# An attention part whose TensorE work stands in one fixed pattern per chunk

## The chip, the cores and the metric

The kernel runs on one core of a Trainium2 chip. The metric is device time in microseconds (us), the median of several runs; lower is better. PE is TensorE, DVE VectorE, ACT ScalarE, POOL GpSimd, SP SyncE, which issues nearly all DMAs.

## The reference

Attention over 4 batches, 8 heads, 768 positions and head dimension 64, and a feed-forward layer behind it. A query sees the 96 positions up to its own and the first 8 (the numbers come as inputs), with a penalty by distance whose slope depends on the head:

```
scores = q k^T / 8 - slope[h] * dist        (dist = 96 for a global key that is not local)
scores = where(is_global | is_local, scores, -1e9)
a = exp(scores - max); a = a / (sum(a) + 1e-9)
x = a v                                      (4*768 tokens x 512)
h = x w_in                                   (512 x 2048)
out = (gelu(h)) w_out                        (2048 x 512)
```

The weights come as float64 and are turned into pairs of 32-bit numbers on the chip.

## The kernel before

The program has two parts. The first does the attention, the weights' conversion, and the feed-forward layer for 2 of the 8 slices of 256 hidden units; the second does the other 6 slices with a seven-product scheme (lines 553 and 611). The change is in the first.

The attention goes in 12 chunks of 256 queries, three per batch; the first of a batch is narrow (its first 128 queries see one block of keys), the others wide. A chunk has four pairs of heads. Each step is an entry of a list with a letter, and this is the way of a pair p of chunk c, with its heads h:

- `l` loads q, k and v (tile `nat`); `S` (PE, line 226) makes the scores of both heads. Its matmuls contract over 64 rows of the array, one head on each half. It takes two PSUM banks, one per head.
- `R` (DVE, line 243) adds the penalty and takes the row extreme (`nmax`), out of PSUM into `pn`; `E` (ACT, line 256) is the exponential with its sums; `U` (DVE, lines 262 and 264) is the inverse of the sums (`ninv`); `N` multiplies by it, on DVE, POOL (line 274) or ACT (line 272).
- `T` (PE, line 283) turns the head's blocks with a matmul against the identity, "flips" below; `C` copies the turned blocks out of PSUM (`pt`), on ACT or DVE.
- `A` (PE, line 304) multiplies with v, each head in 64 columns of the array. Two pairs share one bank. `X` and `Y` split the result into a high and a low part (`xh`, `xl`).
- `m` (PE, line 438; line 450 in chunk 0) is the first feed-forward product, 12 matmuls an entry and four entries a chunk; it writes an `h` bank per slice. `G` is the GELU on ACT, `K` its low part on DVE. `n` (PE, line 474) is the second product, 6 matmuls an entry and four a chunk, into two `o` banks; `O` copies those out.
- Beside this run the weights' steps `w`, `D`, `F`, `j`, `J`, `H`, `L`, `Q`, `h`, `o`, `B` (load, low bits, shift, join, round, high and low parts, sums, store), on ACT, DVE, POOL and SP.

The trace shows each matmul of `S` and of `A` as two records, so a pair's scores are 8 records and its V products 16 (12 in a narrow chunk).

What sets the order: `schedule()` plans all entries at build time, with a duration for each engine written in the list. It always places the entry that can start first; on PE, entries that are ready within `SLACK` of each other go by a key (`KEYS`, by chunk and pair), on the other engines by due times with small shifts (`NUDGE`, `BIAS`). There are 8 PSUM banks, shared by the classes `ks` (scores), `kt` (flips), `ka` (V products), `kh` and `ko`; `CAP` says how many a class may hold, `KEEP` how many the planner leaves free for each of the others. The result is one order for all instructions, in which each engine's instructions are then written; on the chip, an engine that waits holds up all that is behind it. In the second part the keys of PE's entries are `strict`: they go in just that order.

Of the kernel before, what the change touches and what calls it, by code (L numbers as in the profile page):

```python
# [26 lines left out]
NST = 8  # L27
# [37 lines left out]
def slope(h):  # L65
# [10 lines left out]
BIAS = {("POOL", "N"): -0.649, ("POOL", "J"): -0.767, ("POOL", "L"): -0.258, ("POOL", "Q"): -0.723, ("POOL", "o"): 0.987, ("POOL", "D"): 0.298,  # L76
        ("ACT", "C"): -0.32, ("ACT", "X"): -0.532, ("ACT", "D"): -0.292, ("ACT", "H"): -0.564, ("ACT", "O"): 0.599, ("ACT", "N"): -0.47}
BIAS_FRONT = {("POOL", "N"): -0.845, ("POOL", "J"): -0.4, ("POOL", "L"): -0.546, ("POOL", "Q"): -0.235, ("POOL", "o"): -0.065, ("POOL", "D"): -0.221,
              ("ACT", "C"): -0.331, ("ACT", "X"): -1.028, ("ACT", "D"): -1.155, ("ACT", "H"): -0.348, ("ACT", "O"): -0.845, ("ACT", "N"): -0.4}
# [9 lines left out]
NUDGE = {("E", 1): -4.66, ("U", 1): 0.08, ("N", 2): -0.21, ("C", 0): 1.4, ("C", 2): -9.57, ("X", 2): 0.57,  # L89
         ("X", 3): -3.65, ("Y", 2): -3.14, ("K", 0): -1.28, ("K", 3): 2.23, ("H", 0): 2.88, ("L", 0): 1.38,  # L90
         ("D", 1): 1.2}
DEC = {(s, i): 57.774 + 7.137 * (4 * (s - NA) + i) for s in range(NA, NST) for i in range(4)}
EARLY_KEYS = {("A", 1): -0.91, ("m", 2): -0.43}
KEYS = {
    "S": lambda g: g + -1.051 + EARLY_KEYS.get(("S", g // 4), 0.0),
    "T": lambda g: g + 0.62 + EARLY_KEYS.get(("T", g // 4), 0.0),
    "A": lambda g: g + 2.296 + EARLY_KEYS.get(("A", g // 4), 0.0),
    "m": lambda c, s: 4 * c + 5.994 + 0.626 * s + EARLY_KEYS.get(("m", c), 0.0),
    "n": lambda c, s: 4 * c + 8.948 + 0.4 * s + EARLY_KEYS.get(("n", c), 0.0),
}  # L100
# [12 lines left out]
class Fast:  # L113
# [559 lines left out]
    def first_part(self):  # L673
# [2 lines left out]
            op(("P", h), [("DVE", .37), ("POOL", .54)], lambda e, h=h: self.penalties(e, h), [("lim",)], port=True)  # L676
        op(("lim",), ("DVE", 1.6), lambda e: self.reach_of_limits(), [("l", 0, 0)], free=[("nat", (0, 0))], port=True)
        lag = KEYS
        for c in range(NCH):
            f = c % CPB == 0  # L680
            for p in range(NP):
                g = 4 * c + p
                y = [("Y", c, p // 2)] if c >= 2 else [("Y", c, p)]
                op(("l", c, p), ("SP", ISSUE), lambda e, c=c, p=p: self.load(c, p), alloc=[("nat", (c, p))],
                   kb=(384, 640)[not f])
                op(("S", c, p), ("PE", (1.06, .86)[f]), lambda e, c=c, p=p: self.scores(c, p), [("l", c, p)],
                   alloc=[("k", ("s", c, 2 * p)), ("k", ("s", c, 2 * p + 1))], key=lag["S"](g))
                for h in (2 * p, 2 * p + 1):
                    op(("R", c, h), ("DVE", (.7, .56)[f]), lambda e, c=c, h=h: self.reduce(c, h), [("S", c, p), ("P", h)],
                       alloc=[("pn", (c, h))], free=[("k", ("s", c, h))])  # L690
                    op(("E", c, h), ("ACT", (.986, .88)[f]), lambda e, c=c, h=h: self.exps(c, h), [("R", c, h)])
                if p % UNITE == UNITE - 1:
                    q = p - UNITE + 1
                    op(("U", c, p // UNITE), ("DVE", .29), lambda e, c=c, q=q: self.inverse(c, q),
                       [("E", c, h) for h in range(2 * q, 2 * p + 2)])
                for h in (2 * p, 2 * p + 1):
                    op(("N", c, h), [("DVE", (.53, .47)[f]), ("POOL", (1.0, .85)[f]), ("ACT", (.8, .71)[f])],
                       lambda e, c=c, h=h: self.scale(e, c, h), [("U", c, p // UNITE)], port=True)
                    op(("T", c, h), ("PE", (.4, .29)[f]), lambda e, c=c, h=h: self.flip(c, h), [("N", c, h)],
                       alloc=[("k", ("t", c, h))], free=[("pn", (c, h))], key=lag["T"](g) + .001 * (h % 2))  # L700
# [3 lines left out]
                op(("A", c, p), ("PE", (1.02, .77)[f]), lambda e, c=c, p=p: self.av_pair(c, p),  # L704
                   [("C", c, 2 * p), ("C", c, 2 * p + 1), ("l", c, p), self.at("A", c, p - 1)],
                   alloc=([("k", ("a", c, p // 2))] if p % 2 == 0 else []) + ([("x", c)] if p == 0 else []),
                   free=[("pt", (c, 2 * p)), ("pt", (c, 2 * p + 1)), ("nat", (c, p))], key=lag["A"](g))
# [54 lines left out]
        for c in range(NCH):  # L762
            for s in range(NA):
# [6 lines left out]
                           free=[("x", c)], key=lag["m"](c, s) + (.01 * p if s else .6 * (p - 3)))  # L770
                    continue
                for f in range(2):
                    op(("m", c, s, f), ("PE", 1.5), lambda e, c=c, s=s, f=f: self.m1(c, s, f),
                       ys + [("L", s, 0), ("L", s, 1), self.at("m", c, s, 0)] , alloc=[("k", ("h", c, s))] if f == 0 else [],
                       free=[("x", c)], key=lag["m"](c, s) + .01 * f)
            for batch in BATCH(c):
                op(("G",) + batch[0], ("ACT", 1.02 * len(batch)), lambda e, batch=batch: self.gelu(batch),
                   [("m",) + b + (3 if c < SPLIT else 1,) for b in batch], alloc=[("g", b) for b in batch])
# [1 line left out]
                    op(("K",) + b, ("DVE", .6), lambda e, b=b: self.gelu_low(*b), [("G",) + batch[0]], free=[("k", ("h",) + b)])  # L780
            for s in range(NA):
                for k in range(2):
                    op(("n", c, s, k), ("PE", 1.4), lambda e, c=c, s=s, k=k: self.m2(c, s, k),
                       [("K", c, s), ("L", s, 2), ("L", s, 3), ("H", s, 3), self.at("n", c, s - 1, k)],
                       alloc=[("k", ("o", c, k))] if s == 0 else [], free=[("g", (c, s))], key=lag["n"](c, s) + .01 * k)
# [210 lines left out]
    def schedule(self):  # L996
# [95 lines left out]
                make_ready(i)  # L1092
        self.start, self.on = [None] * n, [None] * n
        port = pipe = 0.0
        self.uses_port = uses_port = lambda o, e: e == "POOL" or e == "DVE" and o.port
        while len(done) < n:
            best = None
            for e in engines:
                found, low = [], None
                k = 0  # L1100
                for i in ready[e]:
# [16 lines left out]
                    if low is None or t < low:  # L1118
                        low = t
                    found.append((t, i))  # L1120
# [311 lines left out]
```

## Time and profile before

| | us |
|---|---|
| median of 3 runs (669.45 to 670.78) | 669.74 |
| the profiled execution | 670.06 |
| its span, first to last instruction | 668.30 |
| PE busy in the span | 647.85 |
| first product of the second part starts at | 288.85 |

The span is what the trace covers; the profiled execution's time has another 1.8 us around it. The starts of PE's instructions are measured, their ends modelled: a row's busy time can reach past the next row's start.

### The profile page before, as it was taken

How to read it: one execution, taken by the hardware profiler on the slowest of the kernel's cores; microseconds unless marked ns; L12 is line 12 of the kernel's file. 1: busy time of each engine (PE TensorE's matmuls, PEld its weight loads, DVE VectorE, ACT ScalarE, POOL GpSimd, SP SyncE). 2: the span in 40 equal slices, each digit the busy share in tenths (PEclk: the TensorE clock that was granted, in tenths of full speed). 3: DMA queues.
4: the chain of work that ended last, by engine and by line, in shares of the span. 5: the costliest groups of instructions: out<-in, count | busy, mean ns of one | idle time of the engine just before them, and what ended most of it. 6: DMA issues, size and time to landing. Idle time of an engine off the chain costs nothing. (4 is left out here: it accounts for less than half of the span.)

```text
span 668.3 us, 14910 instructions
## 1 busy us (share of the span) xinstructions
PE 647.9 (97%) x5356; PEld 593.7 (89%) x5356; DVE 544.7 (82%) x1562; ACT 443.5 (66%) x1146; POOL 178.1 (27%) x216
## 2 busy tenths in 40 slices
PE   8999999999999999999999999999999999999994
PEld 6778878777887887899999999999999999999994
DVE  8998799999899977366588879778977987897784
ACT  6999999899999988445554465456445545644450
POOL 5667776765786553200000000000000000000002
PEclk9999999999999999999999999999999999999998
DMA  8876798689898869969997879688888979787302
GB/s 317 286 234 198 284 380 301 246 305 366 304 367 310 306 257 402 375 236 351 416 405 265 290 276 389 216 310 310 314 303 290 344 251 334 266 283 248 115 1 69
DMA packets 48753, 192.44 MB, mean 288 GB/s; under 512 B 5408, under 2 KB 5920, under 8 KB 41760
## 3 DMA queue, kind: packets, MB, share of 16 engines
q1 hardware_dynamic: 48384, 191.16, 78.0%
q8 instruction: 44, 0.72, 0.4%
q14 instruction: 37, 0.30, 0.1%
q10 hardware_dynamic: 288, 0.26, 0.1%
HBM read 150.50 MB, written 40.89 MB: 286 GB/s over the span
## 5 line engine op out<-in xcount | busy, mean ns | idle before, releaser
L611 PE MATMUL k<-w,go 128*128 128x256 f32 x1512 | 193.9, 282 | 1.7 <-DVE vw L620 0.8
L611 PEld LDWEIGHTS k<-w,go 128*128 128x128 f32 x1512 | 185.1, 189 | 3.0 <-PE k L553 1.6
L553 PE MATMUL k<-xch,w1a 128*128 128x256 f32 x576 | 110.4, 284 | 0.5 <-DVE hc L563 0.5
L620 POOL TENSOR_TENSOR part<-part,r 128x256 f32<-128x256 f32 x1 | 0.7, 740 | 372.3 <-DVE r L620 372.3
L256 ACT ACTIVATE pn<-pn,nmax 128x256 f32<-128x256 f32 (+1 forms) x192 | 91.8, 480 | 7.0 <-DVE nmax L243 6.7
L553 PEld LDWEIGHTS k<-xch,w1a 128*128 128x128 f32 x576 | 92.5, 191 | 1.0 <-DVE hc L563 0.7
L553 PE MATMUL k<-xch,w1b 128*128 128x256 f32 x432 | 91.4, 282 | 0.5 <-ACT hc L559 0.5
L559 ACT COPY hc<-k 128x256 f32<-128x256 f32 x108 | 39.8, 369 | 68.0 <-PE k L553 67.6
L553 PE MATMUL k<-xcl,w1a 128*128 128x256 f32 x288 | 81.4, 283 | 0.0
L563 DVE TENSOR_TENSOR hc<-hc,k 128x256 f32<-128x256 f32 x108 | 45.0, 417 | 36.1 <-ACT hc L559 26.3
L595 ACT CAST go<-gb 128x384 fp32r<-128x384 f32 x72 | 36.9, 513 | 55.6 <-PE k L611 55.3
L553 PEld LDWEIGHTS k<-xch,w1b 128*128 128x128 f32 x432 | 73.1, 191 | 0.7 <-ACT hc L559 0.7
L243 DVE CUSTOM_DVE_ANT_0 pn<-k,pens 128x256 f32<-128x256 f32 (+1 forms) x192 | 65.7, 395 | 7.5 <-PE k L226 6.6
L571 ACT ACTIVATE gb<-hc 128x256 f32<-128x256 f32 x108 | 45.2, 419 | 40.0 <-DVE hc L563 39.0
L553 PE MATMUL k<-xcl,w1b 128*128 128x256 f32 x216 | 60.9, 282 | 0.0
L272 ACT ACTIVATE pn<-pn,ninv 128x256 f32<-128x256 f32 (+1 forms) x118 | 50.0, 484 | 10.8 <-DVE ninv L264 10.5
L194 DVE TENSOR_TENSOR go<-gb,go 128x384 fp32r<-128x384 f32 x72 | 40.0, 555 | 19.7 <-ACT go L595 19.3
L283 PE MATMUL k<-ident,pn 128*128 128x128 f32 x352 | 51.5, 279 | 4.3 <-DVE pt L191 1.6
L553 PEld LDWEIGHTS k<-xcl,w1a 128*128 128x128 f32 x288 | 55.1, 191 | 0.0
L354 POOL TENSOR_TENSOR wa<-wa,ws 128x512 int32<-128x512 int32 x32 | 44.2, 1383 | 35.9 <-DVE wa L349 15.4
L226 PE MATMUL k<-nat 64*128 64x256 f32 (+1 forms) x384 | 50.8, 384 | 2.8 <-ACT pt L191 0.8
L438 PE MATMUL k<-xh,winh 128*128 128x256 f32 x176 | 52.3, 297 | 0.8 <-DVE xl L194 0.8
(122 smaller groups left out, 1464.1 us busy)
## 6 DMA issues: line engine op xcount, KB each, us to landing
w1a<-w1d SPq DMA_DIRECT2D x36, 1024.0 KB, 7.4
w1b<-w1d SPq DMA_DIRECT2D x36, 768.0 KB, 5.1
nat<-qkv SPq DMA_DIRECT2D x32, 640.0 KB, 5.9
ws<-w SPq DMA_DIRECT2D x32, 512.0 KB, 5.4
c<-w SPq DMA_DIRECT2D x64, 256.0 KB, 5.3
w1d<-wst SPq DMA_DIRECT2D x6, 1792.0 KB, 6.7
w2d<-wst SPq DMA_DIRECT2D x6, 1792.0 KB, 6.5
nat<-qkv SPq DMA_DIRECT2D x16, 386.0 KB, 4.6
```

What stands on the lines that cost most here:

```text
L194: self.eng(e).tensor_tensor(out=out, in0=in_, in1=hi.bitcast(F32), op=ALU.subtract)
L226: self.nc.tensor.matmul(sp[hh][:, j, :w], lhsT=qq[hr, j * P:(j + 1) * P], rhs=kt[hr, 0 if first else j, :w], start=True, stop=True)
L243: self.nc.vector.tensor_tensor_reduce(out=nn[:, j, :w], in0=sp[:, j, :w], in1=pen, scale=-0.125, scalar=3e38, op0=ALU.add, op1=ALU.min, ac ...
L256: self.nc.scalar.activation(out=nn[:, j, :w], in_=nn[:, j, :w], func=AF.Exp, bias=self.nmax[:, k, i:i + 1], scale=-1.0, accum_out=self.nsu ...
L272: self.nc.scalar.activation(out=nn[:, j, :w], in_=nn[:, j, :w], func=AF.Copy, scale=by)
L283: self.nc.tensor.transpose(tp[:, i, :], nn[:, j, a * P:(a + 1) * P], self.ident)
L354: self.eng(e).tensor_tensor(out=a, in0=a, in1=self.t["ws", (s, i)][:, :, 0], op=ALU.add)
L438: nc.tensor.matmul(hp[:, f, :], lhsT=w[:, d, f * P:(f + 1) * P], rhs=x[:, d, :], start=n == 0, stop=n == 3 * NP - 1)
L553: self.nc.tensor.matmul(out, lhsT=w[:, i, d * P:(d + 1) * P], rhs=y[:, d, :], start=bool(new) and n == 0, stop=n == 5, skip_group_check=no ...
L563: self.nc.vector.tensor_tensor(out=x, in0=x, in1=self.t["k", (bank, u)], op=ALU.add)
L571: self.nc.scalar.activation(out=out, in_=src, func=AF.Gelu)
L611: self.nc.tensor.matmul(out[k], lhsT=o[:, i, a], rhs=w[:, b, j], start=s == 0 and n == 0 and k in (1, 4, 5, 6), stop=s == NB - 1 and n == ...
```

## The change

It does four things to the planner and none to the matmuls. `turn(x, y)` gives a time that PE loses between an entry of kind x and one of kind y; the planner adds it to an entry's earliest start on PE, and the durations of S, T, A, m and n in the list become smaller. `SEATS` gives each S, T, A, m and n a place in a chunk's period of 4, and in the keys from 10.086 to 44.882 (`STEADY`) these entries are strict. `KEEP` becomes zero throughout and scores may hold four banks. The tables of shifts have new numbers (only some are shown).

```diff
-CAP = {"ks": 2, "kt": 3, "ka": 2, "kh": 2, "ko": 2, "kb": 4}
-KEEP = {"ks": 1, "kt": 1, "ka": 1, "kh": 1, "ko": 3}
+CAP = {"ks": 4, "kt": 3, "ka": 2, "kh": 2, "ko": 2, "kb": 4}
+KEEP = {"ks": 0, "kt": 0, "ka": 0, "kh": 0, "ko": 0}
...
-FRONT = 26.926
-SPLIT, CHECK, UNITE, RING = 1, 8, 1, 3
+FRONT = 8.503
+SPLIT, CHECK, UNITE, RING, GREED = 1, 8, 1, 3, 0.0
+STEADY = (10.086, 44.882)
+SEATS = {"S": [-2.0, -1.84, 0.0, 0.16],
+         "T": [0.4, 0.48, 0.56, 0.64, 1.85, 2.56, 2.64, 2.93],
+         "A": [1.6, 1.76, 3.6, 3.76],
+         "m": [4.45, 4.53, 4.61, 4.69],
+         "n": [7.2, 7.28, 7.44, 8.44]}
...
-DEC = {(s, i): 57.774 + 7.137 * (4 * (s - NA) + i) for s in range(NA, NST) for i in range(4)}
+DEC = {(s, i): 57.774 + 6.435 * (4 * (s - NA) + i) for s in range(NA, NST) for i in range(4)}
...
+def turn(x, y):
+    if x == y:
+        return .08 if x == "T" else 0.0
+    if x == "T":
+        return {"S": .175, "A": .175, "m": .07, "n": .11}.get(y, .08)
+    if x in ("S", "A"):
+        return {"S": .2, "A": .1}[x] + {"T": .055, "m": .09, "n": .125}.get(y, 0.0)
+    if x in ("m", "n"):
+        return {"S": .09, "A": .09}.get(y, 0.0)
+    return 0.0
...
+        def seat(kind, c, k, free):
+            at = 4 * c + SEATS[kind][k]
+            return dict(key=at, strict=True) if STEADY[0] <= at < STEADY[1] else dict(key=free)
+
...
-                op(("S", c, p), ("PE", (1.06, .86)[f]), lambda e, c=c, p=p: self.scores(c, p), [("l", c, p)],
-                   alloc=[("k", ("s", c, 2 * p)), ("k", ("s", c, 2 * p + 1))], key=lag["S"](g))
+                op(("S", c, p), ("PE", (.86, .66)[f]), lambda e, c=c, p=p: self.scores(c, p), [("l", c, p)],
+                   alloc=[("k", ("s", c, 2 * p)), ("k", ("s", c, 2 * p + 1))], **seat("S", c, p, lag["S"](g)))
...
-                op(("A", c, p), ("PE", (1.02, .77)[f]), lambda e, c=c, p=p: self.av_pair(c, p),
+                op(("A", c, p), ("PE", (.92, .71)[f]), lambda e, c=c, p=p: self.av_pair(c, p),
...
+                    if e == "PE":
+                        base = max(base, free[e] + turn(turned, o.name[0]))
...
+                    late = GREED * turn(turned, o.name[0]) if e == "PE" else 0.0
...
+            if e == "PE":
+                turned = o.name[0]
```

With these numbers the order of PE changes throughout the first part. In a seated chunk it is now: two pairs of S, three flips, three n, two pairs of A, two pairs of S, a flip, the last n, then m and a flip in turn (m, T, m, T, m, T, m), two pairs of A, a flip. Before, the chunks differ from each other. The first place is PE at the second V products of a chunk, with `k` the PSUM banks, `nat` the loaded pair, `pn` the scaled exponentials and `pt` their turned copies. Before, where chunk 3 ends and chunk 4's scores stand:

```order
L304 MATMUL k_1371<-pt_1379,nat_1035 64x128
...
L304 MATMUL k_1371<-pt_1396,nat_1035 64x128
L226 MATMUL k_1429<-nat_1314 128x256
L226 MATMUL k_1430<-nat_1314 128x256
L226 MATMUL k_1429<-nat_1314 128x256
L226 MATMUL k_1430<-nat_1314 128x256
L283 MATMUL k_1442<-ident,pn_1343 128x128 x4
L474 MATMUL k_1383<-wouth_644,gh_1_1306 128x512
```

One pair of A, one pair of S, a flip, and an entry of n. Now, at the like place (the lines are 20 or so further down in the changed file: 246 is S, 303 T, 324 A, 494 n):

```order
L324 MATMUL k_1422<-pt_1340,nat_989 64x128
...
L324 MATMUL k_1422<-pt_1411,nat_998 64x128
L246 MATMUL k_1449<-nat_1322 128x256
L246 MATMUL k_1450<-nat_1322 128x256
L246 MATMUL k_1449<-nat_1322 128x256
L246 MATMUL k_1450<-nat_1322 128x256
L246 MATMUL k_1460<-nat_1324 128x256
L246 MATMUL k_1461<-nat_1324 128x256
L246 MATMUL k_1460<-nat_1324 128x256
L246 MATMUL k_1461<-nat_1324 128x256
L303 MATMUL k_1471<-ident,pn_1349 128x128 x4
L494 MATMUL k_1388<-wouth_594,gh_1_1309 128x512
```

Two pairs of A (`nat_989` and `nat_998`) and two pairs of S stand together, and four banks of scores are open at once. The second place is PE at a block of scores near entries of n. Before, a pair of chunk 4 stands behind an entry of n, ahead of flips and m:

```order
L474 MATMUL k_1402<-wouth_644,gh_1_1306 128x512
L226 MATMUL k_1491<-nat_1351 128x256
L226 MATMUL k_1492<-nat_1351 128x256
L226 MATMUL k_1491<-nat_1351 128x256
L226 MATMUL k_1492<-nat_1351 128x256
L283 MATMUL k_1503<-ident,pn_1398 128x128 x4
L283 MATMUL k_1513<-ident,pn_1413 128x128 x4
L438 MATMUL k_1521<-xh_1292,winh_463 128x256
```

Now, at the first two pairs of chunk 5, the block has two pairs again, with flips on both sides and three entries of n in a run behind them:

```order
L303 MATMUL k_1644<-ident,pn_1487 128x128 x4
L246 MATMUL k_1650<-nat_1444 128x256
L246 MATMUL k_1651<-nat_1444 128x256
...
L246 MATMUL k_1661<-nat_1455 128x256
L246 MATMUL k_1662<-nat_1455 128x256
L303 MATMUL k_1675<-ident,pn_1494 128x128 x4
L303 MATMUL k_1681<-ident,pn_1517 128x128 x4
L303 MATMUL k_1689<-ident,pn_1549 128x128 x4
L494 MATMUL k_1697<-wouth_468,gh_0_1619 128x512
```

What moved: S and A pairs of a chunk have come together in twos, and the flips between m and m are one at a time. From the first product of the second part on, PE's rows are the same in both.

## Rows read from the trace of the kernel before

**Rows 1.** Busy time by stretch: from:to, length, each engine (records), clock, DMA share, GB/s.
```profile
0.00:62.50 62.50, 57.94 (x487) 46.59 (x489) 56.28 (x206) 54.84 (x155) 40.46 (x60) 1.00 0.75 256
62.50:253.90 191.40, 186.73 (x1548) 151.89 (x1548) 173.98 (x506) 179.42 (x488) 125.18 (x140) 1.00 0.84 313
253.90:288.80 34.90, 34.80 (x282) 29.92 (x277) 20.94 (x58) 22.33 (x59) 8.88 (x12) 1.00 0.97 371
288.80:668.30 379.50, 368.39 (x3051) 365.27 (x3050) 293.48 (x796) 186.87 (x446) 3.56 (x5) 0.99 0.75 273
sum 668.30, PE 647.85 PEld 593.67 DVE 544.68 ACT 443.47 POOL 178.08; mean PE 161.96 PEld 148.42 DVE 136.17 ACT 110.87 POOL 44.52
```

**Rows 2.** Timeline of PE: start, busy us, line, output and inputs, array, shape, records.
```profile
4.70 1.58 PE L226 MATMUL k<-nat 64*128 64x128 f32 x16
6.99 0.93 PE L226 MATMUL k<-nat 64*128 64x128 f32 x8 [0.71 <-DMA nat<-qkv]
...
101.45 0.36 PE L438 MATMUL k<-xh,winh 128*128 128x256 f32 x1
...
102.97 0.60 PE L283 MATMUL k<-ident,pn 128*128 128x128 f32 x4
103.32 0.36 PE L438 MATMUL k<-xh,winh 128*128 128x256 f32 x1
...
104.93 1.14 PE L226 MATMUL k<-nat 64*128 64x256 f32 x8
106.00 1.09 PE L304 MATMUL k<-pt,nat 128*64 128x128 f32 x16
107.02 1.09 PE L283 MATMUL k<-ident,pn 128*128 128x128 f32 x8
108.04 1.14 PE L226 MATMUL k<-nat 64*128 64x256 f32 x8
...
110.13 0.50 PE L474 MATMUL k<-wouth,gh 128*128 128x512 f32 x1
...
110.93 0.40 PE L474 MATMUL k<-wouth,gh 128*128 128x512 f32 x1
...
182.87 1.97 PE L304 MATMUL k<-pt,nat 128*64 128x128 f32 x32
...
283.10 0.28 PE L438 MATMUL k<-xh,winh 128*128 128x256 f32 x1
...
288.85 0.28 PE L553 MATMUL k<-xch,w1a 128*128 128x256 f32 x1
```

**Rows 3.** Groups by line and shape, 62.5 to 253.9: busy us, mean ns, idle before.
```profile
L272 ACT ACTIVATE pn<-pn,ninv 128x256 f32<-128x256 f32 x75 | 33.7, 499 | 5.0 <-DVE ninv L264 4.9
L339 ACT ACTIVATE ws<-ws 128x512 int32<-128x512 uint32 x17 | 11.2, 672 | 0.0
L191 ACT COPY pt<-k 128x512 f32<-128x512 f32 x15 | 8.3, 578 | 1.1 <-PE k L283 1.1
L243 DVE CUSTOM_DVE_ANT_0 pn<-k,pens 128x256 f32<-128x256 f32 x106 | 39.8, 416 | 4.7 <-PE k L226 4.2 <-ACT pn L256 0.3 <-PE k L283 0.2
L191 DVE COPY pt<-k 128x512 f32<-128x512 f32 x27 | 18.0, 682 | 2.8 <-PE k L283 2.8
L400 DVE TENSOR_TENSOR wst<-wa,wst 128x512 fp32r<-128x512 f32 x7 | 7.0, 999 | 0.0
L274 POOL TENSOR_SCALAR pn<-pn,ninv 128x256 f32<-128x256 f32 x29 | 14.8, 521 | 16.3 <-DVE ninv L264 8.4 <-ACT pn L256 5.6 <-PE k L226 2.0
```

**Rows 4.** Busy time by stretch, two chunks, columns as in rows 1.
```profile
136.10:160.30 24.20, 21.77 (x185) 17.48 (x185) 23.16 (x69) 21.91 (x64) 13.05 (x14) 1.00 0.89 340
183.60:207.70 24.10, 24.10 (x218) 20.07 (x216) 23.38 (x67) 23.83 (x64) 16.59 (x18) 1.00 0.88 340
```

**Rows 5.** Waits of ACT, 62.5 to 253.9: us in total, times, longest.
```profile
ACT pn L272 <- DVE ninv L264: 8.5, 10, 1.8
```

**Rows 6.** Waits of PE, 136.1 to 160.3.
```profile
PE k L283 <- DVE pt L191: 1.4, 2, 0.9
```

More of the change, by code (lines that the diff above doesn't have):

```diff
@@ L72 @@
          "hc1": 2, "hc6": 2, "hc5": 2, "gb0": 5, "gb1": 7, "gx": 2}
-CAP = {"ks": 2, "kt": 3, "ka": 2, "kh": 2, "ko": 2, "kb": 4}
-KEEP = {"ks": 1, "kt": 1, "ka": 1, "kh": 1, "ko": 3}
+CAP = {"ks": 4, "kt": 3, "ka": 2, "kh": 2, "ko": 2, "kb": 4}
+KEEP = {"ks": 0, "kt": 0, "ka": 0, "kh": 0, "ko": 0}
 SOON, SLACK, WINDOW, LAT, LAT0, IDLE = 0.0, 0.1, 12, 0.255, .05, 19.761
[L76 to L79, printed above, removed]
-FRONT = 26.926
-SPLIT, CHECK, UNITE, RING = 1, 8, 1, 3
+BIAS = {("POOL", "N"): -1.029, ("POOL", "J"): -0.767, ("POOL", "L"): 0.15, ("POOL", "Q"): -0.723, ("POOL", "o"): 0.987, ("POOL", "D"): 0.852,
+        ("ACT", "C"): -0.32, ("ACT", "X"): -0.657, ("ACT", "D"): -0.292, ("ACT", "H"): -0.564, ("ACT", "O"): 0.279, ("ACT", "N"): -0.527}
+BIAS_FRONT = {("POOL", "N"): -0.807, ("POOL", "J"): -0.4, ("POOL", "L"): -0.546, ("POOL", "Q"): -0.235, ("POOL", "o"): -0.065, ("POOL", "D"): -0.221,
+              ("ACT", "C"): -0.331, ("ACT", "X"): -1.028, ("ACT", "D"): -1.155, ("ACT", "H"): -0.479, ("ACT", "O"): -0.845, ("ACT", "N"): -0.256}
+FRONT = 8.503
[6 more added lines that the diff above has]
+         "n": [7.2, 7.28, 7.44, 8.44]}
 W2_AFTER = {(3, 1): ("p", 1, 1), (4, 0): ("p", 1, 4), (4, 1): ("p", 2, 4), (5, 0): ("p", 3, 4), (5, 1): ("p", 4, 4)}
@@ L88 @@
 FREE = (3.4, 2.5, 3.0, 2.0, .8)
-NUDGE = {("E", 1): -4.66, ("U", 1): 0.08, ("N", 2): -0.21, ("C", 0): 1.4, ("C", 2): -9.57, ("X", 2): 0.57,
-         ("X", 3): -3.65, ("Y", 2): -3.14, ("K", 0): -1.28, ("K", 3): 2.23, ("H", 0): 2.88, ("L", 0): 1.38,
-         ("D", 1): 1.2}
-DEC = {(s, i): 57.774 + 7.137 * (4 * (s - NA) + i) for s in range(NA, NST) for i in range(4)}
-EARLY_KEYS = {("A", 1): -0.91, ("m", 2): -0.43}
+NUDGE = {("R", 2): -2.16, ("R", 3): 4.48, ("E", 0): -3.31, ("E", 1): -4.66, ("E", 3): 1.13, ("U", 2): 0.06,
[4 rows of a table added]
+DEC = {(s, i): 57.774 + 6.435 * (4 * (s - NA) + i) for s in range(NA, NST) for i in range(4)}
+EARLY_KEYS = {("A", 1): -0.91, ("A", 3): -0.65, ("m", 1): -0.46, ("m", 2): -0.43, ("n", 0): -0.23, ("n", 2): -1.11}
 KEYS = {
-    "S": lambda g: g + -1.051 + EARLY_KEYS.get(("S", g // 4), 0.0),
+    "S": lambda g: g + -1.156 + EARLY_KEYS.get(("S", g // 4), 0.0),
     "T": lambda g: g + 0.62 + EARLY_KEYS.get(("T", g // 4), 0.0),
@@ L98 @@
     "m": lambda c, s: 4 * c + 5.994 + 0.626 * s + EARLY_KEYS.get(("m", c), 0.0),
-    "n": lambda c, s: 4 * c + 8.948 + 0.4 * s + EARLY_KEYS.get(("n", c), 0.0),
+    "n": lambda c, s: 4 * c + 9.246 + 0.4 * s + EARLY_KEYS.get(("n", c), 0.0),
 }
@@ L698, in first_part @@
                        lambda e, c=c, h=h: self.scale(e, c, h), [("U", c, p // UNITE)], port=True)
-                    op(("T", c, h), ("PE", (.4, .29)[f]), lambda e, c=c, h=h: self.flip(c, h), [("N", c, h)],
-                       alloc=[("k", ("t", c, h))], free=[("pn", (c, h))], key=lag["T"](g) + .001 * (h % 2))
+                    op(("T", c, h), ("PE", (.36, .25)[f]), lambda e, c=c, h=h: self.flip(c, h), [("N", c, h)],
+                       alloc=[("k", ("t", c, h))], free=[("pn", (c, h))], **seat("T", c, h, lag["T"](g) + .001 * (h % 2)))
                     op(("C", c, h), [("ACT", (.49, .39)[f]), ("DVE", (.6, .47)[f])],
@@ L703, in first_part @@
                        [("T", c, h)], alloc=[("pt", (c, h))], free=[("k", ("t", c, h))])
[L704 removed]
+                op(("A", c, p), ("PE", (.92, .71)[f]), lambda e, c=c, p=p: self.av_pair(c, p),
                    [("C", c, 2 * p), ("C", c, 2 * p + 1), ("l", c, p), self.at("A", c, p - 1)],
                    alloc=([("k", ("a", c, p // 2))] if p % 2 == 0 else []) + ([("x", c)] if p == 0 else []),
[L707 removed]
+                   free=[("pt", (c, 2 * p)), ("pt", (c, 2 * p + 1)), ("nat", (c, p))], **seat("A", c, p, lag["A"](g)))
                 if c < 2:
@@ L772, in first_part @@
                 for f in range(2):
-                    op(("m", c, s, f), ("PE", 1.5), lambda e, c=c, s=s, f=f: self.m1(c, s, f),
+                    op(("m", c, s, f), ("PE", 1.44), lambda e, c=c, s=s, f=f: self.m1(c, s, f),
                        ys + [("L", s, 0), ("L", s, 1), self.at("m", c, s, 0)] , alloc=[("k", ("h", c, s))] if f == 0 else [],
-                       free=[("x", c)], key=lag["m"](c, s) + .01 * f)
+                       free=[("x", c)], **seat("m", c, 2 * s + f, lag["m"](c, s) + .01 * f))
             for batch in BATCH(c):
@@ L782, in first_part @@
                 for k in range(2):
-                    op(("n", c, s, k), ("PE", 1.4), lambda e, c=c, s=s, k=k: self.m2(c, s, k),
+                    op(("n", c, s, k), ("PE", 1.36), lambda e, c=c, s=s, k=k: self.m2(c, s, k),
                        [("K", c, s), ("L", s, 2), ("L", s, 3), ("H", s, 3), self.at("n", c, s - 1, k)],
-                       alloc=[("k", ("o", c, k))] if s == 0 else [], free=[("g", (c, s))], key=lag["n"](c, s) + .01 * k)
+                       alloc=[("k", ("o", c, k))] if s == 0 else [], free=[("g", (c, s))], **seat("n", c, 2 * s + k, lag["n"](c, s) + .01 * k))
             for k in range(2):
@@ L1094, in schedule @@
         port = pipe = 0.0
+        turned = ""
         self.uses_port = uses_port = lambda o, e: e == "POOL" or e == "DVE" and o.port
@@ L1117, in schedule @@
                         continue
-                    if low is None or t < low:
-                        low = t
-                    found.append((t, i))
+                    late = GREED * turn(turned, o.name[0]) if e == "PE" else 0.0
+                    if low is None or t + late < low:
+                        low = t + late
+                    found.append((t + late, i, t))
                     k += 1
@@ L1125, in schedule @@
                     continue
-                t, i = next((t, i) for t, i in found if t <= low + SLACK)
+                t, i = next((t, i) for late, i, t in found if late <= low + SLACK)
                 if best is None or t < best[0]:
```

4 rows, old and new, of the table NUDGE are left out of this document.

## The prediction

> **What bounds the kernel now.** I read the table of busy time by stretch first [rows 1]. Over the span PE is busy 647.85 of 668.30 us, DVE 544.68, ACT 443.47. Its four stretches say where these meet: up to 62.5 us (chunks 0 to 2), 62.5 to 253.9 (from the first exponential of chunk 3 to that of chunk 11, eight chunks), 253.9 to 288.8 (the rest of the attention part), and the second part. In the eight chunks PE idles only 4.7 of 191.4 us, but ACT is busy 179.4 (93.7%) and DVE 174.0 (90.9%). In the stretch behind them ACT works 22.3 of 34.9 us; in the second part ACT and DVE are far from full. So PE is the bound, with ACT right behind it just where the change has most of its effect.
>
> A busy PE is not a PE at its peak, and that difference is what the change is about. The timeline of PE gives starts; from start to start is what an operation costs the engine [rows 2]. A pair's V products alone take 1.02 us (106.00 to 107.02) and are busy 1.09; two pairs in one row are busy 1.97. The second adds 0.88, so a lone pair pays some 0.15 for itself. Two narrow pairs of scores in one row are busy 1.58, one alone 0.93: the second adds 0.65. A score block's modelled end lies 0.07 behind the next start (1.14 busy, 104.93 to 106.00), so the lone one costs 0.86 and pays 0.20 for itself. The neighbours pay too. Twelve records of m take 1.61 us ahead of scores (103.32 to 104.93) and 1.52 ahead of a flip (101.45 to 102.97): 0.09 for whoever stands ahead of S or A. The first n behind A is busy 0.50, a later one like it 0.40: 0.10 for an n, and I take the same for an m. Among flips, m and n nothing is lost: 48 records of m in a run take 5.75 us (283.10 to 288.85), so twelve 1.44; with four flips between m and m they take 1.87 (101.45 to 103.32), which leaves 0.108 a flip, no more than eight flips have between A and S (1.02).
>
> So S (64 rows of the array) and A (64 columns) are islands with a price at each shore. The Trainium skill, Perfetto Trace Analysis, Identifying the Most-Contended Engine, says that matmul busy share is a bad measure of headroom and the weight loads' share a good one. The trace agrees with the first half: PE's idle time in the eight chunks is 4.7 us, while the shores counted below hold 17.8. By the second half 39 us would be open there (weight loads 151.9 of 191.4 us); the starts decide, and they give less.
>
> **The change, part by part.** It moves instructions; no matmul is added or taken away. I counted blocks in the order of PE's instructions, of before and of the change, up to the second part's first product. Blocks of S fall from 45 to 25: 20 x 0.20 = 4.0 us. Blocks of A fall from 43 to 27: 16 x 0.15 = 2.4. Blocks of flips, m or n ahead of S or A fall from 62 to 37: 25 x 0.09 = 2.3. Blocks of m or n right behind S or A fall from 27 to 5: 22 x 0.10 = 2.2. Flips there hardly change (35 to 34, 0.1). Sum 11.0 us of PE's time (25.4 before, 14.4 after); by stretch it is 0.5 in chunks 0 to 2, 8.9 in the eight chunks (17.8 to 8.9), 1.6 behind them. The second part's matmuls stand in the same order, so it starts earlier and keeps its length.
>
> The other engines' work hardly changes in total. By the order ACT loses 40 scalings of pn (40 x 0.499 = 20.0 us) and takes 26 copies out of PSUM (18 turned tiles, four o, four wide xh: 26 x 0.578 = 15.0 at most) and six low-bit conversions (6 x 0.672 = 4.0): -1.0 us [rows 3]. POOL takes these scalings (40 x 0.521 = 20.8) and gives up six conversions and eleven subtractions, about as much. DVE gives up the 26 copies (26 x 0.682 = 17.7 at most) and takes ten subtractions (at most 10 x 0.999): about -8. So ACT keeps its 179.4 us in the eight chunks. Where PE would be done in 191.4 - 8.9 = 182.5 us, ACT would have to be busy 98.3%. That term decides.
>
> Its bounds from the rows: the fullest chunk of before has ACT busy 23.83 of 24.10 us, 98.9% [rows 4]; the whole stretch has 93.7%. At 93.7% nothing is gained in the eight chunks; at 98.9% all of PE's 8.9 is. I take the middle, 96.3%: 179.4 / 0.963 = 186.3 us, a gain of 5.1. For more than 93.7% speaks that 8.5 of ACT's 12 idle us lie ahead of scalings that wait for the inverse from DVE [rows 5], and a third of ACT's scalings go. In chunks 0 to 2 and behind chunk 10 ACT has room, so 0.5 and 1.6 stand. Sum: 5.1 + 0.5 + 1.6 = 7.2 us. Against the profiled execution's own 670.06 us (span 668.30 and 1.8 around it) that gives 662.9; the median of the runs is 669.74, 0.3 lower, and from it the forecast is 662.5.
>
> Other edits. The planner's new durations only move the plan. Loads, spills and stores of the attention part change places on SP's queue, and the weights' due times come earlier (6.435 us apart, not 7.137). It is the same DMAs, at a share of 0.84 in the eight chunks and 0.97 behind them [rows 1], and the last ones ahead of the second part (xr, w1) keep their order. I cost this at nothing. If the second part's start came before its weights, up to the 7 us gained would be lost again.
>
> The seats are strict: where a seat's operands are late, everything behind it on PE waits, the m and n that could have filled the gap among it, and then ACT and DVE wait for PE.
>
> **The rivals.** (1) PE gets it all, ACT packing as in its fullest chunk. For it: DVE loses 8 us, so inverses can come sooner. Against it: one chunk of eight reaches that share now. 669.74 - 11.0 = 658.7 us.
>
> (2) ACT gives little: at 95% in the eight chunks (188.8 us, 2.6 gained) and 2.1 outside them, 665.0; at 93.7%, 667.6. For it: ACT's waits come from chains over three engines that the change doesn't shorten.
>
> (3) Slower, by PSUM banks. There are 8, and the planner no longer reserves any. Two pairs of scores together take four. At the block behind the first A pairs, two h banks, one of A and one of a flip fill the rest; at the other block two o banks stand in place of h. The flips, n or m behind a score block then get a bank only when DVE has reduced a head's scores (two instructions of 0.416 us and their read-outs [rows 3]), and DVE is busy 90.9%. What such a chunk costs shows in before: from 136.1 to 160.3 PE idles 2.4 us [rows 4], most of it waiting for DVE's copies out of PSUM [rows 6]. At 2.4 us in each of nine seated chunks the waits are 21.9 in place of 4.7: 669.74 - 11.0 + 17.2 = 676 us. It decides from (11.0 + 4.7) / 9 = 1.7 us of waiting per chunk. Against it: a wide score block of two pairs lasts about 1.9 us, in which DVE can reduce the first two heads.
> The Trainium skill, TensorEngine Tiling (Array Packing), PSUM Bottleneck, points the same way: tiling speeds up TensorE but not the emptying of PSUM. The rows named in this rival agree as far as they go.
>
> (4) The islands don't cheapen as counted, since a second wide pair of scores pays as the first does (no row shows two wide pairs together): 4.0 us less for PE, 7.0 gained in rival 1's case, 662.7. With ACT as the bound the forecast stays.
>
> **How the numbers follow.** What a measurement of this kernel can tell from no change is about 0.2%, 1.3 us. Chances: the forecast, with 3.7 to 10 us gained, 0.47 (its own range 659.7 to 666.0; rival 4 lies in it); rival 1, 10 us or more, 0.20; rival 2 with 1.3 to 3.7 us, 0.13; no change, 0.08; slower, rival 3, 0.12. So faster 0.80, same 0.08, slower 0.12. The range goes from 657.8 (rival 1 and one us of PE's waits gone) to 669.6, just short of no gain; slower cases and a few beyond 12 us stay out.
>
> **What would show it.** In the profile after, two wide pairs of scores take about 1.9 us from start to start, two of A 1.89, and a seated chunk has four islands. The eight chunks are shorter by 0.6 us each, with ACT's share near 96% and PE's idle time up from 4.7 to 8 or 9 us, its waits on ACT or DVE. The second part takes 379.5 us again. The forecast is wrong if PE's idle time there stays below 5 us (rival 1) or passes 15 (rival 3, then on flips, n and m right behind a score block), or if the second part grows.

## The result and the profile after

The changed kernel takes 659.69 us (median of 6 runs, 659.44 to 660.11), against 670.12 for the kernel before in as many runs: 0.9842 of its time, 95% interval 0.9829 to 0.9855. The gain is 10.4 us; 7.2 were forecast. The profiled execution takes 660.07 us, its span 658.30.

The busy time by stretch, of the kernel after, with borders at the same events as in [rows 1] (first exponential of chunk 3, of chunk 11, first product of the second part) and the same columns:

```profile
0.00:62.80 62.80, 57.92 (x495) 48.25 (x496) 56.53 (x213) 55.51 (x153) 41.70 (x64) 1.00 0.74 256
62.80:245.60 182.80, 179.66 (x1530) 152.88 (x1529) 163.03 (x488) 179.00 (x481) 133.33 (x158) 1.00 0.87 320
245.60:279.30 33.70, 33.70 (x287) 30.19 (x287) 18.07 (x54) 24.22 (x62) 8.46 (x13) 1.00 1.01 399
279.30:658.30 379.00, 368.31 (x3051) 365.27 (x3049) 293.47 (x795) 186.99 (x446) 3.55 (x5) 0.99 0.75 275
```

The second part starts at 279.3 instead of 288.8 and is 379.0 instead of 379.5 long, so 9.5 of the 10 us between the two spans come from the attention part, and 8.6 of these from the eight chunks (191.4 to 182.8). There ACT is busy 179.0 us, as before (179.4), but now in 97.9% of the stretch. PE idles 3.1 us, not 4.7. DVE lost 11 us of work; POOL got 8.2 more.

PE's timeline after: start, busy us, line (246 is S, 303 T, 324 A), shape, records. One island of chunk 4's V products and chunk 5's scores:

```profile
113.77 1.97 PE L324 MATMUL k<-pt,nat 128*64 128x128 f32 x32
115.67 2.00 PE L246 MATMUL k<-nat 64*128 64x256 f32 x16
117.60 0.66 PE L303 MATMUL k<-ident,pn 128*128 128x128 f32 x4
```

From start to start that is 1.90 us for two pairs of A and 1.93 for two wide pairs of S; 1.89 and about 1.9 were forecast. A lone wide pair cost 1.06 and more [rows 2]. Of the fourteen blocks of two wide pairs of S ten take 1.93, and none over 2.00.

The groups of the eight chunks after that answer to [rows 3], 62.8 to 245.6: records, then busy us, mean ns, idle before.

```profile
L292 ACT ACTIVATE pn<-pn,ninv 128x256 f32<-128x256 f32 x45 | 21.0, 502 | 1.0 <-DVE ninv L284 1.0
L359 ACT ACTIVATE ws<-ws 128x512 int32<-128x512 uint32 x22 | 14.3, 681 | 0.0
L211 ACT COPY pt<-k 128x512 f32<-128x512 f32 x25 | 14.0, 588 | 1.5 <-PE k L303 1.3
L263 DVE CUSTOM_DVE_ANT_0 pn<-k,pens 128x256 f32<-128x256 f32 x104 | 39.3, 418 | 1.7 <-PE k L246 1.5
L211 DVE COPY pt<-k 128x512 f32<-128x512 f32 x17 | 11.5, 682 | 1.6 <-PE k L303 1.6
L294 POOL TENSOR_SCALAR pn<-pn,ninv 128x256 f32<-128x256 f32 x59 | 33.6, 582 | 15.7 <-DVE ninv L284 9.7 <-ACT pn L276 2.8 <-PE k L324 2.4
```

Thirty wide scalings left ACT for POOL, and ACT took copies and conversions for them. What ACT waits for in the same stretch (us in total, times, longest) answers to [rows 5]:

```profile
ACT pt L211 <- PE k L303: 1.5, 3, 0.9
ACT pn L292 <- DVE ninv L284: 1.0, 1, 1.0
```

The wait of the scalings for the inverse of the sums fell from 8.5 us to 1.0. That is the larger part of the 8.2 us that ACT's idle time lost (12.0 to 3.8). PE's waits there are all short:

```profile
PE k L494 <- DVE nmax L263: 0.9, 1, 0.9
PE k L303 <- ACT pt L211: 0.5, 1, 0.5
PE k L303 <- DVE o L211: 0.4, 1, 0.4
```

**Where PE's time went.** I divided PE's time up to the second part, start by start, into the price of each block's own work, the shores (blocks counted in the order, times the prices of the prediction) and the rest, which is waiting and the warming-up of PE before its first scores. Own work went from 248.6 to 249.2 us, shores from 25.4 to 14.4, the rest from 13.7 to 14.6: 0.6 - 11.0 + 0.9 = -9.5 us. On this sum the shores account for the whole result. It is worked out from prices, so the 11.0 in it is the count and not a measurement. The idle time that the rows show for PE up to the second part fell from 9.3 to 8.0 us, while the rest rose: ends are modelled, and some waiting lies inside busy rows. Twelve records of flips behind two pairs of scores take 1.39 us from start to start at 106.85, but 1.65 at 174.77, with an idle time of only 0.12.

### The profile page after: what moved, and what is told of

It reads as the page before. It is cut to its first block, busy times and chain, and to the rows that moved or that the text cites. A ratio compares the mean times of both kernels' runs of the same rounds, so it can differ in the third digit from the quotient of the medians.

```text
span 658.3 us, 14879 instructions
## 1 busy us (share of the span) xinstructions
PE 639.6 (97%) x5359; PEld 596.6 (91%) x5359; DVE 531.1 (81%) x1546; ACT 445.7 (68%) x1141; POOL 187.0 (28%) x239
## 5 line engine op out<-in xcount | busy, mean ns | idle before, releaser
L294 POOL TENSOR_SCALAR pn<-pn,ninv 128x256 f32<-128x256 f32 (+1 forms) x114 | 62.1, 560 | 31.6 <-DVE ninv L284 18.6
L303 PEld LDWEIGHTS k<-ident,pn 128*128 128x128 f32 x352 | 38.4, 140 | 13.5 <-issue 4.6
```

Of the source, the lines that this page charges most:

```text
L294: self.eng(e).tensor_scalar(out=nn[:, j, :w], in0=nn[:, j, :w], scalar1=by, scalar2=0.0, op0=ALU.mult, op1=ALU.add)
L303: self.nc.tensor.transpose(tp[:, i, :], nn[:, j, a * P:(a + 1) * P], self.ident)
```

## The experiments

The theory: the gain is that of the shores, and ACT, full behind PE, limits what more can come through. The rivals: the new tables of shifts brought it; the places of the weights' steps brought it; or PE was not the bound and ACT's lost waits were. In this section "the eight chunks" always lie between the same two exponentials, and a window's columns are those of [rows 1]. An experiment that takes one thing out of the change keeps tables that were chosen for the whole of it, so its loss can overstate what that thing brings. The change's bank limits (`CAP`, `KEEP`) and its shorter durations were not undone by themselves.

**Tables alone.** The kernel before with the tables of the change:

```diff
-BIAS, BIAS_FRONT, FRONT, NUDGE, DEC, EARLY_KEYS, KEYS of before
+those of the change
```

> The kernel before with the tables and due times of the change, but no turning costs, no seats, and before's durations and bank rules. PE has 25.4 us of shores, as before; ACT has 92 scalings in place of 118. Theory 1 (shores): within 2 us of before, 668 to 672. Theory 2 (fewer scalings on ACT): 662 to 665.

Measured 670.27 us, 1.0002 of before (0.9993 to 1.0012): nothing. The shores stay at 25.4 us.

```profile
0.00:68.20 68.20, 61.19 (x509) 49.60 (x509) 63.12 (x212) 59.60 (x160) 45.02 (x65) 1.00 0.73 253
68.20:254.60 186.40, 184.67 (x1512) 150.38 (x1512) 166.41 (x499) 175.11 (x473) 117.92 (x145) 1.00 0.90 330
```

The eight chunks are 5.0 us shorter, but begin 5.7 later than before: what they gain there is lost ahead of them. This is also a warning against reading a gain from one stretch. ACT has fewer scalings here, 68 in place of 92 in the eight chunks, and still waits for the inverse:

```profile
ACT pn L274 <- DVE ninv L266: 6.5, 5, 2.9
```

**No seats.** The changed kernel with its turning costs and its bank limits, but with no strict places:

```diff
-STEADY = (10.086, 44.882)
+STEADY = (0.0, 0.0)
```

> The changed kernel with no seats (no entry strict in the first part); turning costs, tables and bank rules as changed. By its order of PE: S in 29 blocks, A in 36, so 18.4 us of shores by the prices of the prediction, where the change has 14.4. Theory 1 (PE's shores are the gain): 4.0 us slower than the change's 659.7, so 663.7. Theory 2 (the gain comes from ACT, whose scalings went to POOL and no longer wait): ACT has 88 scalings here, nearly as few as the change's 78, so within 1.5 us of the change. Theory 3 (the fixed pattern as such keeps the engines fed, whatever the shores): 666 or more.

Measured 661.80 us (0.9873; 0.9857 to 0.9889), 2.1 above the change, between theory 1 (663.7) and theory 2 (661.2 at most). The count from the order gives 29 blocks of S and 36 of A, 18.4 us of shores. So a planner that knows what a border costs, together with the new bank limits and set beside the tables alone, takes 7.0 of the 11.0 us of shores away and 8.5 of the 10.6 us of time; the seats bring the other 4.0 and 2.1. The profiled execution took 663.54 us, the longest of its four runs. In its eight chunks ACT is not packed as after:

```profile
57.30:242.30 185.00, 181.57 (x1508) 152.57 (x1506) 177.00 (x507) 176.05 (x470) 134.56 (x153) 0.99 0.86 318
```
```profile
ACT pn L292 <- DVE ninv L284: 5.6, 6, 3.3
```

With 66 scalings on ACT in these chunks it waits 5.6 us for the inverse, where the seated order with 60 waits 1.0. And PE, free to put three pairs of scores in a row, waits behind them until DVE, busy with the weights till 177.67, has reduced heads:

```profile
174.38 2.86 PE L246 MATMUL k<-nat 64*128 64x256 f32 x24
179.18 1.91 PE L303 MATMUL k<-ident,pn 128*128 128x128 f32 x8 [1.94 <-DVE nmax L263]
```

This is the wait that rival 3 named, in the kernel that has its bank limits but no seats.

**Islands apart.** The seats stay, but the two pairs of scores of an island are moved apart:

```diff
-SEATS = {"S": [-2.0, -1.84, 0.0, 0.16],
+SEATS = {"S": [-2.0, -1.40, 0.0, 0.50],
```

> The changed kernel with other seats: the second pair of each score block stands one flip or one m further on, all else in the same places. S comes in 43 blocks in place of 25; 21.3 us of shores by the prices, where the change has 14.4. Theory 1: 7.0 us slower than the change, 666.7. Theory 2 (ACT): its work is the same (74 scalings), so 661 at most.

Measured 662.92 us (0.9893; 0.9877 to 0.9910), 3.2 above the change, for 7.0 us more of shores (21.3; 43 blocks of S). That lies between the two expectations. The second part starts 2.8 us later, and PE's accounting shows why it isn't 7: own work the same, shores +7.0, rest -4.2. The window of the eight chunks and PE's longest wait in them (299 is T, 207 a copy in this run's file):

```profile
65.60:249.80 184.20, 183.50 (x1530) 151.69 (x1529) 160.19 (x490) 177.74 (x478) 138.35 (x164) 1.00 0.88 327
```
```profile
PE k L299 <- ACT pt L207: 0.2, 1, 0.2
```

PE idles 0.7 us of 184.2. The dearer borders took the place of waiting first, most likely since operands that were just late are now in time; only then did they lengthen the kernel. Shores are worth their full count only while PE has nothing else to wait for.

**No turning costs.** Seats as in the change, but the planner believes that a border is free:

```diff
 def turn(x, y):
+    return 0.0
```

> The changed kernel with all turning costs zero in the planner, seats kept. PE's order has 15.3 us of shores (26 blocks of S, 29 of A). Theory 1: 1.0 us slower than the change, 660.7: the planner's knowledge of neighbours matters only by the order that it makes. Rival: without it the plan is wrong by 14 us in PE's time, other engines are planned too early, and waits bring it to 664 or more.

Measured 665.54 us (0.9934; 0.9917 to 0.9950), 5.8 above the change, with 15.3 us of shores, only 0.9 more. PE's waits in the eight chunks:

```profile
66.20:250.20 184.00, 175.92 (x1516) 150.38 (x1515) 164.30 (x483) 176.60 (x473) 132.57 (x159) 1.00 0.86 312
```
```profile
PE k L304 <- DVE gl L215: 2.1, 3, 0.9
PE k L495 <- ACT pn L277: 1.2, 1, 1.2
PE k L247 <- DMA nat<-qkv: 1.1, 1, 1.1
```

PE idles 8.1 us instead of 3.1, and the chunks begin 3.4 us later. The rival of this expectation held (664 or more): it isn't enough that the order has fewer borders, the plan must allow for them. The reason is argued: where PE's plan runs ahead of the chip, the other engines' steps are put in an order that PE doesn't keep, and strict places turn this into waits. The run leaves the shorter durations of the change in place, so its plan lacks the borders altogether; whether seats with the durations of before, in which a border is contained on average, would do as well was not run.

**Old tables and old due times.** The change with two tables of shifts and the due times of before, and with the due times alone. `BIAS_FRONT`, which the first expectation names too, stays as in the change, and so do `FRONT` and the keys:

```diff
-BIAS, NUDGE of the change                      (first kernel only)
+those of before
-DEC = {(s, i): 57.774 + 6.435 * ...            (both kernels)
+DEC = {(s, i): 57.774 + 7.137 * ...
```

> The changed kernel with the tables of before (BIAS, BIAS_FRONT, NUDGE, DEC), seats, turning costs and bank rules kept. 14.9 us of shores, ACT has 94 scalings where the change has 78 and before 118. Theory 1: about 0.5 us slower than the change by shores, and ACT a little fuller: 660 to 662. Theory 2 (fewer scalings on ACT are the gain): 94 of them lie 40% of the way back, about 4 us slower, 664.

> The changed kernel with one line of before: the weights' due times 7.137 us apart in place of 6.435. PE's blocks and shores up to the second part are those of the change (14.4 us). Theory A (the earlier due times keep the second part from waiting for its weights, as the run with all old tables suggests, whose second part took 385.2 us, 6 more): second part 383 to 386, total 663 to 666. Theory B (that was an effect of the other tables): second part 379, total 659 to 661.

Measured 665.45 us (0.9928; 0.9912 to 0.9945) and 660.00 us (0.9839; 0.9821 to 0.9858). In both the second part starts earlier than in the change, at 278.6 and 276.1, and is longer, 385.2 and 382.3 us. The old tables, eight chunks and second part, and the second part with old due times:

```profile
64.50:245.20 180.70, 179.78 (x1563) 155.66 (x1562) 152.04 (x481) 179.72 (x485) 139.06 (x157) 1.00 0.85 314
278.60:663.80 385.20, 371.12 (x3051) 367.65 (x3049) 295.11 (x797) 189.72 (x451) 3.55 (x5) 0.99 0.76 280
```
```profile
276.10:658.40 382.30, 370.20 (x3051) 366.68 (x3049) 293.35 (x795) 187.67 (x447) 3.54 (x5) 0.99 0.77 279
```

ACT is fuller in the eight chunks of the old tables than in those of any other kernel with the whole work: 99.5%, with 68 scalings and no wait for the inverse. So that ACT gave scalings away is not why its waits went; with the same 68, the tables alone wait 6.5 us. The loss is in the second part, and neither theory of the first expectation had named it. The waits of PE over the span, old tables and then old due times:

```profile
PE k L629 <- DVE go L212: 3.2, 1, 3.2
...
PE k L571 <- DMA w1a<-w1d: 1.9, 1, 1.9
```
```profile
PE k L631 <- ACT go L615: 1.8, 1, 1.8
```

and what those engines had waited for there, in the same two kernels:

```profile
DVE gx L598 <- DMA pd<-o: 3.3, 1, 3.3
ACT go L613 <- DMA pd<-o: 2.2, 1, 2.2
```
```profile
DVE gx L600 <- DMA pd<-o: 2.3, 1, 2.3
...
ACT go L615 <- DMA pd<-o: 1.6, 1, 1.6
```

The transfers at the start of the second part come late. The same transfers are issued ahead of it in all three kernels, but when it starts 88.1 MB have been moved in the change, 85.9 with old due times and 84.7 with old tables. The early due times make the attention part 3.2 us longer and the second part 3.3 shorter; the one cancels the other, and 0.3 us between the medians is no difference. Which transfer or step of the attention part costs the 3.2 was not taken apart.

**Lighter engines.** To see which engine binds, part of the work was left out. ACT light leaves out the second part of GELU in chunks 2 to 11, 8 us of ACT in the eight chunks; PE light leaves out the products of the weights' high part with `xl` in m, 21 us of PE, 15 of it in the eight chunks. The edits, in before and in the change:

```diff
-            nc.scalar.activation(out=hp, in_=hp, func=AF.Gelu)
+            if c < 2:
+                nc.scalar.activation(out=hp, in_=hp, func=AF.Gelu)
...
-            for w, x in ((wh, xh), (wh, xl), (wl, xh)):
+            for w, x in ((wh, xh), (wl, xh)):
```

> The kernel before, without the second GELU of chunks 2 to 11 (the one that feeds the low part): 20 instructions of about 0.505 us start to start, 8.1 us of ACT in the eight chunks; the order is the same. Theory 1 (PE is the bound of before, ACT has 12 us of idle time): at most 2 us faster, from the few waits of PE for ACT. Theory 2 (ACT is the bound): 8 us faster, 662.

> The kernel before, without the product of the high weights with xl in m of chunks 1 to 11: 176 matmuls of 0.12 us, 21.1 us of PE, 15.4 of them in the eight chunks; the order of the rest is the same. Theory 1: PE gives its time back until ACT is full: 12 us of ACT's idle time there at most, and about 4 in the rest: 12 to 16 us faster, 654 to 658. Theory 2 (ACT): only the rest, 4 to 6 us faster.

> The changed kernel without the second GELU of chunks 2 to 11, 8.1 us of ACT in the eight chunks, order the same. Theory 1 with PE still the bound: 1 to 3 us faster than the change (PE's waits in the eight chunks are 6 us in all), 657 to 659. Rival (ACT has become the bound, at 97.9% busy): 5 to 8 us faster, 652 to 655.

> The changed kernel without the product of the high weights with xl in m of chunks 1 to 11, 21.1 us of PE, 15.4 in the eight chunks. If ACT is full beside PE there (3.8 us idle): 3.8 + about 4 outside = 7 to 9 us faster than the change, 651 to 653. If PE alone bounds: 17 to 21 us faster, 639 to 643.

> The changed kernel without the second GELU of chunks 2 to 11 and without the product of the high weights with xl in m of chunks 1 to 11: 8.1 us less of ACT and 15.4 less of PE in the eight chunks, order the same. Alone, ACT's cut shortened the eight chunks by 1.4 us, PE's by 2.3. Theory: each alone meets the other engine, which is full; both together give 8 to 10 in the eight chunks and 5 more behind them, total 645 to 649. Rival (neither is the bound, but the chain from scores over DVE and ACT back to PE): about the sum, 4 in the eight chunks, total 652 to 655.

| | us | ratio to before, 95% interval | saved |
|---|---|---|---|
| before, ACT light | 667.64 | 0.9971 (0.9959 to 0.9982) | 2.0 to 2.5 |
| before, PE light | 663.61 | 0.9914 (0.9897 to 0.9930) | 6 |
| after, ACT light | 658.72 | 0.9831 (0.9814 to 0.9847) | 1.0 |
| after, PE light | 655.43 | 0.9792 (0.9774 to 0.9810) | 4.3 |
| after, both | 652.13 | 0.9729 (0.9713 to 0.9746) | 7.6 |

The eight chunks of each, in the order of the table:

```profile
62.30:252.10 189.80, 185.48 (x1534) 151.29 (x1534) 173.00 (x504) 171.53 (x471) 125.41 (x140) 1.00 0.85 313
```
```profile
62.30:250.40 188.10, 174.12 (x1421) 136.59 (x1417) 174.98 (x507) 178.61 (x487) 125.47 (x140) 1.00 0.85 319
```
```profile
63.10:244.50 181.40, 178.82 (x1527) 152.11 (x1526) 162.36 (x486) 171.88 (x466) 133.56 (x158) 1.00 0.88 320
```
```profile
62.60:243.10 180.50, 167.57 (x1403) 137.83 (x1402) 161.87 (x488) 178.43 (x483) 133.25 (x158) 1.00 0.89 326
```
```profile
63.00:240.20 177.20, 166.62 (x1398) 136.93 (x1397) 161.09 (x486) 171.56 (x465) 133.13 (x158) 1.00 0.89 331
```

The PE-light kernel of before was the largest miss: theory 1 expected 12 to 16 us, and 6 came, as much as theory 2 (ACT as the bound) had allowed. With 15 us less to do in its eight chunks PE idles 14.0 us there, and yet ACT reaches only 178.61 of 188.10, 95.0%, and waits as before:

```profile
ACT pn L272 <- DVE ninv L264: 8.3, 8, 1.8
```

In before's order ACT's 94 to 95% was thus set by that order, not by PE. After the change the PE-light kernel has ACT busy 98.9%, and there it ends (7 to 9 us were expected, 4.3 came). With both lighter neither engine is full: PE idles 10.6 us, ACT 5.6, and 5.6 us are gained in the eight chunks where the two alone gain 1.4 and 2.3. The total of 652.13 lies in the rival's range (652 to 655), not in the theory's (645 to 649). That the two gain more together than apart shows two bounds side by side; that they don't gain all shows the chains between engines behind them.

**Searched tables.** The last run looks for a better version: the change with seats a few tenths apart (one gap between islands closed) and other shifts:

```diff
-         "T": [0.4, 0.48, 0.56, 0.64, 1.85, 2.56, 2.64, 2.93],
+         "T": [0.19, 0.49, 0.6, 0.66, 1.3, 2.46, 3.2, 2.92],
...
-(BIAS, BIAS_FRONT, NUDGE, EARLY_KEYS of the change)
+(others, found by search)
```

> The changed kernel with only its tables of numbers replaced: seats moved by some tenths (the fifth flip of a chunk from 1.85 to 1.30, which closes one gap between islands), other preferences of engines, shifts and early keys, found by searching for a shorter plan. Counted from the order: shores 13.5 in place of 14.4 us (-0.9); ACT takes some 15 wide scalings more and gives up some 12 copies of turned tiles and two unpacking steps, in total within half a us of before. Theory 1 (after the change PE and ACT are both full, their idle time in the eight chunks being 3.1 and 3.8 us, so only counted work is left to gain): 0 to 1 us shorter than the changed kernel, 658.7 to 659.7. Rival (most of what the change gave was a plan whose waits fit the chip, so a better plan gives more than its shores, out of the 5 us of waiting in the first three chunks and the 3 us in the eight): 2 to 4 us shorter, 655.7 to 657.7. Third (the plan is fitted to its own durations and falls behind on the chip, as the plan without turning costs did): longer than 660.5, with PE's idle time in the eight chunks over 4 us or the second part longer than 380.

Measured 657.77 us (0.9819; 0.9806 to 0.9833): faster than both kernels, 1.9 us below the change, just outside the rival's 655.7 to 657.7 and well beyond theory 1. Its eight chunks and second part:

```profile
65.40:244.40 179.00, 174.36 (x1518) 150.63 (x1517) 165.36 (x490) 173.67 (x471) 130.91 (x152) 1.00 0.88 326
278.50:656.40 377.90, 368.44 (x3050) 365.24 (x3049) 293.30 (x795) 187.13 (x446) 3.57 (x5) 0.99 0.75 275
```

The second part starts 0.8 us earlier. That is as much as the 0.9 us of shores, but not shown to be them: PE idles 4.6 us in the eight chunks, 1.5 more than in the change. Another 1.1 us come from a second part of 377.9 us, but not from PE's work in it: from its first to its last product PE takes 371.4 us here and 370.9 in the change. What is shorter is the tail behind PE's last product, 6.6 us in place of 8.0, at whose end only the last stores of `out` are under way. Tails from 6.6 to 8.3 us appear in the kernels with the whole work; why they differ stays open.

## Why the prediction was right, and where it was not

**The count of PE's shores was right.** The prices hold for islands that no row had shown: 1.93 us for two wide pairs of scores, 1.90 for two of A. So rival 4 fell. Blocks times prices gave 11.0 us, and the second part's start shows 9.5 of them; by the division above waits grew by 0.9 and other work by 0.6. That the tables alone gave nothing and that moving the pairs apart again cost 3.2 us speaks for the shores, too.

**ACT's work was right, its share was not.** The forecast held ACT at 179.4 us in the eight chunks, and it is 179.0, by just the trade that was counted: scalings out, copies and conversions in. The step that failed is the next: "I take the middle, 96.3%". ACT reaches 97.9%, so the eight chunks take 182.8 us instead of 186.3, a gain of 8.6 instead of 5.1. These 3.5 us are what the forecast missed; the median's gain is 3.2 us larger than forecast. Nor was ACT's share the term that decides: with 7.1 us less for ACT to do (ACT light, 171.88 of 181.40) the eight chunks of the change are only 1.4 us shorter, and PE is full beside it (98.3% busy). The ends, 93.7 and 98.9%, were shares of the order that the change replaces. The PE-light run of before shows that its lower end came from that order's own waits, which stay when PE is relieved; the old tables on the seated order pass the upper end, 99.5%. A middle between them said nothing on the new order.

**Its reason was half right.** The waits for the inverse did go (8.5 to 1.0 us), but not, as the prediction had it, because a third of the scalings leave ACT. With about 68 in the eight chunks the kernels without seats wait 6.5 and 5.6 us, the seated one 0. A lighter DVE isn't the reason by itself: it is busy 89.3% in the tables alone and 89.2% in the change, which wait 6.5 and 1.0. So it is the regular order that brings the inverse in time, and it must fit the plan: the seated kernels with islands apart and without turning costs, with 54 and 58 scalings, wait 2.3 and 2.8. That the spacing of a chunk's steps does it is argued from there, and no run took it apart.

**By its own mark, rival 1 came.** The prediction said that a PE idle time below 5 us would mean that PE gets it all, and put 0.20 on it; 8 to 9 us were forecast, 3.1 are measured, and the time is 1 us from that rival's 658.7. The range held the time because rival 1 lay in it; the likeliest case's own range, 659.7 to 666.0, only touches it.

**Outside the eight chunks.** The 0.5 us of chunks 0 to 2 does not show (62.5 to 62.8): PE idles 0.3 us more there and has eight more records ahead of that border, three of them of its warming-up. Behind chunk 10 1.2 of the 1.6 came. Stretches cut at another engine's instruction are not the same work twice; the sum is.

**Due times at nothing** held as a sum, 0.3 us in the run that undoes them alone, but it is 3.2 us lost and 3.3 gained. The condition named there, a second part that starts before its weights, is in part what the old tables ran into: their second part is 6.2 us longer, and PE's waits there are 1.9 us for `w1a` and 3.2 behind the stores of `o` (`pd`).

**Other engines.** DVE lost 11 us in the eight chunks, 8 were forecast. POOL was to give up as much as it takes and got 8.2 us more; its wide scalings rose from 29 to 59 and from 521 to 582 ns each. It still idles 49 us of the stretch.

**Rival 3 did not come.** With four banks of scores open the seated chunks wait 3.1 us in all, not 2.4 each [rows 4, 6]; DVE, 11 us lighter, reduces the first heads within the two-pair block, and the waits on `nmax` sum to 1.4 us. The Trainium skill, TensorEngine Tiling (Array Packing), PSUM Bottleneck, warns that tiling does not speed up the emptying of PSUM; the trace shows little of it here, at most these 3.1 us. The wait that the rival named does occur: 1.94 us in one place without seats, behind three pairs of scores. That strict seats can turn into waits is shown by the run without turning costs: 8.1 us of PE's idle time and 5.8 us of time, though its rows don't tell banks from late operands.

**PE's room.** The prediction decided by starts and not by weight loads (the second half of the rule of the Trainium skill, Perfetto Trace Analysis, Identifying the Most-Contended Engine, by which 30 us would be open even now: 152.88 of 182.80). The islands-apart run agrees with the starts: weight loads at 151.69 of 184.20 us, and no more than 0.7 us of PE idle.

## What to carry to other kernels

Where an array is switched between forms, read the price of a border from start to start, count borders in the order, and give the price to whatever plans the order: here the planner that knew it, with its new bank limits, brought most of the gain, and the same seats without it lost more than half. Don't take the second engine's fullest share under the old order as its ceiling under a new one; look at what its idle time waits for, and whether relieving the first engine makes it go. And follow a moved start through the next stage: a second part that starts early can wait for its data.

## What the chip showed beside

A short wait of PE can cost more than its length. In the old-tables kernel PE waits 3.2 us at the start of the second part (PE's timeline, start, busy us):

```profile
304.21 1.86 PE L629 MATMUL k<-w,go 128*128 128x256 f32 x7 [3.17 <-DVE go L212]
305.87 0.41 PE L571 MATMUL k<-xch,w1b 128*128 128x256 f32 x1
306.08 0.41 PE L571 MATMUL k<-xcl,w1b 128*128 128x256 f32 x1
...
309.60 0.28 PE L571 MATMUL k<-xch,w1b 128*128 128x256 f32 x1
309.71 0.28 PE L571 MATMUL k<-xcl,w1b 128*128 128x256 f32 x1
```
```profile
300.00:310.00 10.00, 6.68 (x35) 6.26 (x34) 4.54 (x13) 3.01 (x7) 0.00 (x0) 0.66 0.97 383
```

Behind it a product takes 0.21 us from start to start until 309.6, then 0.11 to 0.12: the granted clock of these ten us is 0.66, full speed and half of it (2.4 and 1.2 GHz) mixed. Its 25 products from 304.21 on take 5.4 us, some 2.4 more than at 0.12 each. The run without seats has the same behind its wait of 1.94 us: eight flips take 1.84 us from start to start (179.18 to 181.02) where eight took 1.02 [rows 2], and the granted clock from 179.1 to 183.0 is 0.56. Part of the 1.7 us by which that execution lies above its median may be this. The waits of up to 0.9 us in the change's eight chunks have nothing of the kind behind them: the granted clock is 1.00 there.

POOL's wide scaling has no fixed price: 521 ns before, 582 after, 637 with the old due times, 699 with the old tables, with the same shape and type. What slows it was not tested.
